# Low parts of the later batches' weights and keys: from GpSimd to VectorE

## The chip, the cores and the metric

The kernel runs on one core of a Trainium2 chip. The metric is the time of one execution on the device in microseconds (us); lower is better. Engines are named as in the profile: PE is TensorE, DVE is VectorE, ACT is ScalarE, POOL is GpSimd, SP is SyncE, which issues most of the transfers.

## The reference

Four batches of 576 positions pass through three layers one after the other: attention with 8 heads of 64, which keeps only scores close to the row's largest; a channel layer with a low-rank mixing of positions in front of it; and a layer of 8 experts, to which each position is routed.

```python
scores = q @ k.T / sqrt(64)                     # 4 batches, 8 heads, 576 x 576
scores = where(scores >= max(scores) - tau, scores, -1e9)
x = softmax(scores) @ v                         # heads side by side: 576 x 512
u = x + (x.T @ U @ V).T                         # rank 32, over positions
x = u + relu(u @ w_ch1) @ w_ch2                 # 512 -> 2048 -> 512
e[s] = argmax(x @ w_gate) or the expert of the position before   # by x @ w_local
out = p[e] * relu(x @ w1[e]) @ w2[e]            # 512 -> 1024 -> 512
```

All of it is in float32, and the outputs have to stand close to that.

## The kernel before

**High and low parts.** A float32 operand of a matrix product is split in two: `hi` is the value rounded to the format that PE multiplies fast (an ACT copy into a tile of that type), `lo` is the rest, a subtraction `x - hi` on another engine. A product is then three matmuls: hi times hi, hi times lo, lo times hi. Low parts that read a product's result in PSUM are made on DVE (`hl` at line 618). Two kinds of low part read two tiles in SBUF, and stand on POOL: those of the channel layer's weights (`w0l` and `w1l`, line 598, 128x512) and those of the keys (`kl`, line 268, 128x576 and 128x640), the latter but for the first pair of heads, which has them on DVE.

**The loops.** `attention(b)` goes over 4 pairs of heads, and in each over 5 groups of rows. For a group PE makes two tiles of scores `s`, DVE takes their maximum (line 326) and the threshold `st` (line 330, two numbers a row), ACT the exponential (line 337), DVE masks (line 341), and PE transposes the result and multiplies it by the values. `load_pair` brings the next pair's keys and queries. `channel(b)` goes over 16 blocks f of the hidden layer. `mlp_l1` makes `l` tiles of 256 and 320 columns from 12 matmuls each; ACT writes `hh` from one, DVE writes `hl` from it, and then the PSUM bank is free. After each fourth block `mlp_l2` adds four blocks up (lines 631 to 633), and DVE adds the result to `yT` (line 634). `load_w(b, f)` is called two blocks ahead: two transfers, two roundings on ACT (line 597), two low parts on POOL. `w0` has two buffers of each part, `w1` five, the raw `wr` six. The `l` tiles share two PSUM banks with the tiles of the router (`route`: `row`, `bk`, `cnt`) and of the stores (`py`); during the last batch's channel layer every third of them has one of two further banks.

**What runs together.** The first batch's attention runs alone. Then `attention(b)` and `channel(b-1)` are interleaved for b = 1, 2, 3, together with the router and the stores of batch b-2. At the end `channel(3)` runs beside `early_slots`, which sorts the positions of the first three batches by expert (DVE work on small tiles: `ssta`, `oha`, `rha`, and PE's `pia`, line 865, 10 columns). Then come the experts.

**What sets the order.** Nearly all of the program is written as generators, and a scheduler puts each engine's instructions into one static order from its own estimates of their durations; each engine works through its own list in order. Only POOL during the first batch's attention, and SP during the experts, keep the order of the code. `LAST` holds the last `w0l` subtraction; the first gather of the experts, which POOL issues, is put behind it.

Of the kernel before, what the change touches and what calls it, by code (L numbers as in the profile page):

```python
# [8 lines left out]
F32 = mybir.dt.float32  # L9
# [6 lines left out]
ALU = mybir.AluOpType  # L16
# [4 lines left out]
B, H, S, D = 4, 8, 576, 64  # L21
# [62 lines left out]
def attention_channel_moe(ctx, tc, qk, vv, tau, umat, vrep, wch, wgl, wexp, consts, out):  # L84
    nc = tc.nc
    pe, dve, act, pool, sp = nc.tensor, nc.vector, nc.scalar, nc.gpsimd, nc.sync
# [152 lines left out]
    def load_pair(b, hp, later=None):  # L239

        i = b * NPAIR + hp
# [4 lines left out]

        cuts = ((0, 0, 128), (1, 0, S), (0, 704, 832), (1, S, QKW), (0, 128, 704), (0, 832, QKW)) if i == 0 else (
            (1, 0, S), (1, S, QKW), (0, 0, 608), (0, 608, QKW))
        eng = pool if i else dve
        def steps():  # L250
            for n, (kq, c0, c1) in enumerate(cuts):
                c = slice(c0, c1)
# [243 lines left out]
    def attention(b):  # L496
        prev = None
        nxt = load_pair(b, 0)
        for hp in range(NPAIR):
            inp = nxt  # L500
            if hp + 1 < NPAIR:
                nxt = load_pair(b, hp + 1)
            for g in range(5):
                fr = front(b, hp, g, inp)
                yield 1.0
                if prev is not None:
                    yield from with_chain(back(*prev))
                prev = (b, hp, g, inp, fr)
        yield from with_chain(back(*prev))
        while CHAIN:  # L510
            yield link()

    def attention_alone(b):

        pend, debt, loads = [], 0.0, []
        inps = {0: load_pair(b, 0)}
        seq = [(hp, g, h) for hp in range(NPAIR) for g in range(5) for h in range(1 if g == 4 else 2)]
        groups = {}
# [66 lines left out]
    def load_w(b, f):  # L585
        nm = f"{b}_{f}"
        if f >= NF or nm in W:
            return
        while DONE[0] < f:
            next(conv, None)  # L590
        r = []
        for i, bufs in ((0, W0), (1, W1)):
            x = mlp.tile([128, 512], F32, tag="wr", name=f"wr{nm}_{i}", bufs=WR)
            sp.dma_start(out=x, in_=wdram[f * 128:f * 128 + 128, i * 512:i * 512 + 512])
            hi = mlp.tile([128, 512], F32R, tag=f"w{i}h", name=f"w{i}h{nm}", bufs=bufs)
            lo = mlp.tile([128, 512], F32R, tag=f"w{i}l", name=f"w{i}l{nm}", bufs=bufs)
            act.activation(hi, x, AF.Copy)  # L597
            x = pool.tensor_tensor(out=lo, in0=x, in1=hi.bitcast(F32), op=ALU.subtract)  # L598
            if i == 0:
                LAST[:] = [x.ins]  # L600
            r.append((hi, lo))
        W[nm] = r
# [34 lines left out]
    def channel(b):  # L637
        hs = {}
        load_w(b, 0)
        load_w(b, 1)  # L640
        for f in range(NF):
            yield from mlp_l1(b, f, hs)
            if f % 4 == 0 and f:
                yield from mlp_l2(b, f - 4, hs)
            load_w(b, f + 2)
        HS[b] = hs
# [625 lines left out]
```

## Time and profile before

| | us |
|---|---|
| median of 3 runs | 1080.13 (1078.6 to 1081.64) |
| the profiled execution | 1076.96 |
| its span in the trace | 1075.1 |
| first batch's attention alone | up to about 120 |
| attention beside the channel layer | about 120 to 690 |
| last channel layer | about 690 to 790 |
| experts | from about 790 |

A timeline row has start, duration, engine, line, operation, tiles written <- read (buffer numbers left out), the shape where there is one, and the count. In square brackets is the engine's idle time before it and what ended it. A group row has the busy time, the mean duration in ns of one instruction, the idle time just before the group, and who ended that. A row of stretches has the stretch, its length, each engine's busy time with the number of instructions (PE, PEld, DVE, ACT, POOL), the granted PE clock, the share of the DMA engines and GB/s. PEld is the weight load of a matmul and overlaps PE.

### The profile page before, as it was taken

What the parts mean: (1) busy time and instruction counts of PE and PEld (TensorE: products, weight loads), DVE (VectorE), ACT (ScalarE), POOL (GpSimd) and SP (SyncE); (2) the same over time, 40 slices, a digit from 0 to 9 for tenths busy, and PEclk for the clock granted to TensorE, in tenths of its full rate; (3) what the DMA queues carried; (4) which work ended last, traced back from release to release, by engine and by line L of the source; (5) the groups of instructions that cost most, each with busy time, mean ns of one, the idle gap of its engine ahead of it and who ended that gap; (6) DMA issues with size and microseconds to landing.
All of it is one profiled execution on the core that took longest, in us unless ns stands there. A gap on an engine that the chain in (4) does not pass through costs nothing. (4 is left out here: it accounts for less than half of the span.)

```text
span 1075.1 us, 19235 instructions
## 1 busy us (share of the span) xinstructions
PE 1019.5 (95%) x7088; PEld 906.0 (84%) x7088; DVE 678.0 (63%) x1645; ACT 580.3 (54%) x1220; POOL 256.2 (24%) x206
## 2 busy tenths in 40 slices
PE   5789889999999999999899999999999999999996
PEld 4566779888887899888789998989999888988985
DVE  6899766775656566656565654474257865556773
ACT  5788775674656366474645555422245254445563
POOL 1222032241422133042313213213340140120110
PEclk9899999999999999999999999999999999999999
DMA  6645577872423132242312101253124584456650
GB/s 198 198 139 150 156 243 237 253 227 95 129 65 116 54 100 65 76 129 60 111 49 79 50 30 60 88 191 120 59 93 141 176 302 158 160 172 230 201 176 15
DMA packets 57989, 143.80 MB, mean 134 GB/s; under 512 B 7133, under 2 KB 7901, under 8 KB 57888
## 3 DMA queue, kind: packets, MB, share of 16 engines
q1 hardware_dynamic: 54528, 132.27, 39.1%
q0 software_dynamic: 3360, 10.23, 2.8%
q8 instruction: 57, 0.93, 0.3%
q14 instruction: 44, 0.36, 0.1%
HBM read 124.65 MB, written 18.61 MB: 133 GB/s over the span
## 5 line engine op out<-in xcount | busy, mean ns | idle before, releaser
L614 PE MATMUL l<-uh,w0h 128*128 128x256 f32 (+1 forms) x512 | 158.0, 309 | 4.5 <-DVE hl L618 4.1
L631 PE MATMUL l<-hh,w1h 128*128 128x256 f32 (+1 forms) x512 | 157.6, 308 | 0.2 <-DVE exia L814 0.2
L615 PE MATMUL l<-ul,w0h 128*128 128x256 f32 (+1 forms) x512 | 153.3, 299 | 0.0
L616 PE MATMUL l<-uh,w0l 128*128 128x256 f32 (+1 forms) x512 | 153.2, 299 | 0.0
L632 PE MATMUL l<-hl,w1h 128*128 128x256 f32 (+1 forms) x512 | 152.9, 299 | 0.0
L633 PE MATMUL l<-hh,w1l 128*128 128x256 f32 (+1 forms) x512 | 152.6, 298 | 0.0
L598 POOL TENSOR_TENSOR w1l<-wr,w1h 128x512 fp32r<-128x512 f32 x64 | 82.0, 1304 | 281.5 <-ACT w1h L597 242.8
L598 POOL TENSOR_TENSOR w0l<-wr,w0h 128x512 fp32r<-128x512 f32 x64 | 83.4, 1302 | 244.8 <-ACT w0h L597 223.8
L337 ACT ACTIVATE p<-s,st 128x576 f32<-128x576 f32 x144 | 104.4, 740 | 63.0 <-DVE st L326 62.8
L1022 ACT ACTIVATE eh<-ew 128x512 fp32r<-128x512 f32 x160 | 94.1, 627 | 74.3 <-PE el L1138 43.2
L1023 DVE TENSOR_TENSOR el<-ew,eh 128x512 fp32r<-128x512 f32 x160 | 106.5, 691 | 37.9 <-ACT eh L1022 36.4
L341 DVE SCALAR_TENSOR_TENSOR p<-s,st,p 128x576 f32<-128x576 f32 x144 | 114.6, 815 | 16.0 <-ACT p L337 10.4
L326 DVE TENSOR_REDUCE st<-s 128x1 f32<-128x576 f32 x144 | 105.5, 751 | 26.3 <-PE s L293 24.4
L291 PE MATMUL s<-kh,qs 128*128 128x288 f32 x320 | 99.8, 330 | 16.5 <-DVE p L341 6.7
L390 ACT ACTIVATE ptt<-tp 128x512 f32<-128x512 f32 (+1 forms) x192 | 90.2, 492 | 39.9 <-PE tp L389 39.5
L634 DVE TENSOR_TENSOR yT<-l,yT 128x256 f32<-128x256 f32 (+1 forms) x128 | 58.3, 455 | 81.4 <-PE l L633 80.9
L618 DVE SCALAR_TENSOR_TENSOR hl<-l,hh 128x256 fp32r<-128x256 f32 (+1 forms) x128 | 58.1, 454 | 79.3 <-ACT hh L617 78.5
L614 PEld LDWEIGHTS l<-uh,w0h 128*128 128x128 f32 x512 | 97.4, 190 | 7.9 <-DVE hl L618 5.3
L631 PEld LDWEIGHTS l<-hh,w1h 128*128 128x128 f32 x512 | 97.5, 190 | 3.7 <-issue 2.4
L389 PE MATMUL tp<-cst,p 128*128 128x128 f32 x576 | 94.1, 280 | 5.5 <-ACT ptt L390 5.3
L632 PEld LDWEIGHTS l<-hl,w1h 128*128 128x128 f32 x512 | 97.5, 190 | 0.6
L615 PEld LDWEIGHTS l<-ul,w0h 128*128 128x128 f32 x512 | 97.4, 190 | 0.4
(443 smaller groups left out, 2397.6 us busy)
## 6 DMA issues: line engine op xcount, KB each, us to landing
ew<-in_wexp_dram SPq DMA_DIRECT2D x80, 512.0 KB, 4.6
wr<-wdram SPq DMA_DIRECT2D x128, 256.0 KB, 3.0
cr<-in_wch_dram SPq DMA_DIRECT2D x32, 512.0 KB, 5.1
raw<-in_qk_dram SPq DMA_DIRECT2D x30, 304.0 KB, 3.3
wdram<-w SPq DMA_DIRECT2D x32, 256.0 KB, 2.7
v<-in_vv_dram SPq DMA_DIRECT2D x16, 352.0 KB, 3.3
raw<-in_qk_dram SPq DMA_DIRECT2D x16, 320.0 KB, 3.7
raw<-in_qk_dram SPq DMA_DIRECT2D x17, 288.0 KB, 3.3
```

The costliest lines, as they stand in the source:

```text
L291: pe.matmul(s["t"][:, h, :288], lhsT=qs[:, qc:qc + 128], rhs=kh[:, k0:k0 + 288], start=(j == 0), stop=False)
L326: dve.tensor_reduce(out=self.st[:, 0, h:h + 1], in_=self.t[h], axis=AX.XY, op=ALU.max, negate=True)
L337: act.activation(self.halves(h), self.t[h], AF.Exp, bias=self.st[:, 0, h:h + 1])
L341: dve.scalar_tensor_tensor(out=p, in0=self.t[h], scalar=self.st[:, 1, h:h + 1], in1=p, op0=ALU.is_ge, op1=ALU.mult, accum_out=self.rvs[:, ...
L598: x = pool.tensor_tensor(out=lo, in0=x, in1=hi.bitcast(F32), op=ALU.subtract)
L614: pe.matmul(pm, lhsT=w1h[:, wk], rhs=uh[:, k, o:o + n], start=(k == 0), stop=False)
L615: pe.matmul(pm, lhsT=w1h[:, wk], rhs=ul[:, k, o:o + n], start=False, stop=False)
L616: pe.matmul(pm, lhsT=w1l[:, wk], rhs=uh[:, k, o:o + n], start=False, stop=(k == 3))
L631: pe.matmul(pm, lhsT=w2h[:, wd], rhs=hh[:, o:o + n], start=(f == f0), stop=False)
L632: pe.matmul(pm, lhsT=w2h[:, wd], rhs=hl[:, o:o + n], start=False, stop=False)
L633: pe.matmul(pm, lhsT=w2l[:, wd], rhs=hh[:, o:o + n], start=False, stop=(f == f0 + 3))
L1023: dve.tensor_tensor(out=lo, in0=x, in1=hi.bitcast(F32), op=ALU.subtract)
```

## The change

The subtraction that makes a low part is put on DVE in more places. For the weights: all blocks of `channel(1)` and `channel(2)` (2 x 16 blocks x 2 = 64) and the first 8 blocks of `channel(3)` (16), 80 in all; batch 0 and the last 8 blocks stay on POOL. For the keys: the pairs of batches 2 and 3 (2 x 4 pairs x 2 = 16). The instructions themselves, their tiles and their buffers are the same, and so is the last `w0l`, which stays on POOL ahead of the gather.

```diff
@@ load_pair
-        eng = pool if i else dve
+        eng = dve if i == 0 or b > 1 else pool
@@ load_w
-            x = pool.tensor_tensor(out=lo, in0=x, in1=hi.bitcast(F32), op=ALU.subtract)
+            eng = dve if b and (b < B - 1 or f < 8) else pool
+            x = eng.tensor_tensor(out=lo, in0=x, in1=hi.bitcast(F32), op=ALU.subtract)
```

The added line moves all lines behind it by one: line 598 becomes 599, and 618 becomes 619. The scheduler makes new orders. Three places of them follow; in the names `l_1_3_256` is the l tile of batch 1, block 3, columns from 256 on, and `hl_3` the low part of block 3's hidden values; `p_0_4` is pair 0, group 4 of the attention that runs beside it; `l_3_0_1_256` is a tile of batch 3's `mlp_l2`.

DVE where `channel(1)` has come to block 3, in the kernel before (at 336 to 342 us of its trace):

```order
L729 COPY seq_3705<-bk_4006 96x1
L730 SCALAR_TENSOR_TENSOR rsm_3704<-seq_3705,rsm_3704 96x6
L732 TENSOR_TENSOR e_all<-cst,rsm_3704 96x48
L341 SCALAR_TENSOR_TENSOR p_0_4_4078,rv_0_0_3637<-s_0_4_0_4080,st_0_4_4079,p_0_4_4078 128x576
L618 SCALAR_TENSOR_TENSOR hl_3_3971<-l_1_3_0_3972,hh_3_3970 128x256
L733 TENSOR_TENSOR rbig_3706<-e_all,rbig_3706 96x48
L351 TENSOR_SCALAR rv_0_0_3637<-rv_0_0_3637 128x1
L272 SCALAR_TENSOR_TENSOR qs_4141<-raw_2_4152,t_63,qs_4141 64x608
L734 TENSOR_REDUCE rsm_3704<-rbig_3706 96x6
L352 RECIPROCAL rv_0_0_3637<-rv_0_0_3637 128x1
L735 TENSOR_TENSOR tw_all<-rsm_3704 96x6
L618 SCALAR_TENSOR_TENSOR hl_3_3971<-l_1_3_256_4014,hh_3_3970 128x320
```

And DVE there in the changed kernel; the first of the pair's two `kl` stands one row ahead of these:

```order
L730 COPY seq_3705<-bk_4006 96x1
L330 TENSOR_SCALAR st_0_4_4079<-st_0_4_4079,t_63 128x1
L731 SCALAR_TENSOR_TENSOR rsm_3704<-seq_3705,rsm_3704 96x6
L268 TENSOR_TENSOR kl_4143<-raw_1_4148,kh_4142 128x640
L619 SCALAR_TENSOR_TENSOR hl_3_3971<-l_1_3_0_3972,hh_3_3970 128x256
L733 TENSOR_TENSOR e_all<-cst,rsm_3704 96x48
L341 SCALAR_TENSOR_TENSOR p_0_4_4078,rv_0_0_3637<-s_0_4_0_4080,st_0_4_4079,p_0_4_4078 128x576
L734 TENSOR_TENSOR rbig_3706<-e_all,rbig_3706 96x48
L351 TENSOR_SCALAR rv_0_0_3637<-rv_0_0_3637 128x1
L272 SCALAR_TENSOR_TENSOR qs_4141<-raw_2_4152,t_63,qs_4141 64x608
L735 TENSOR_REDUCE rsm_3704<-rbig_3706 96x6
L619 SCALAR_TENSOR_TENSOR hl_3_3971<-l_1_3_256_4014,hh_3_3970 128x320
```

The keys' low parts now stand in DVE's own list. The first `hl_3` has moved ahead of the mask (line 341), and the second stays behind line 272 but ahead of line 352.

DVE in `channel(1)` around block 0, ahead of the low part `hl_0` of columns 256 on, before (at 313 to 316 us):

```order
L341 SCALAR_TENSOR_TENSOR p_0_1_3728,rv_0_0_3637<-s_0_1_0_3730,st_0_1_3729,p_0_1_3728 128x576
L723 TENSOR_SCALAR cr_3721<-row_3720 1x96
L341 SCALAR_TENSOR_TENSOR p_0_1_3728,rv_0_0_3637<-s_0_1_1_3736,st_0_1_3729,p_0_1_3728 128x576
L724 SCALAR_TENSOR_TENSOR cr_3721<-cr_3721,row_3720 1x96
L351 TENSOR_SCALAR rv_0_0_3637<-rv_0_0_3637 128x4
L352 RECIPROCAL rv_0_0_3637<-rv_0_0_3637 128x4
L618 SCALAR_TENSOR_TENSOR hl_0_3680<-l_1_0_256_3747,hh_0_3679 128x320
```

And in the changed kernel:

```order
L599 TENSOR_TENSOR w1l_4_3967<-wr_4_1_3964,w1h_4_3966 128x512
L724 TENSOR_SCALAR cr_3721<-row_3720 1x96
L341 SCALAR_TENSOR_TENSOR p_0_1_3728,rv_0_0_3637<-s_0_1_0_3730,st_0_1_3729,p_0_1_3728 128x576
L725 SCALAR_TENSOR_TENSOR cr_3721<-cr_3721,row_3720 1x96
L341 SCALAR_TENSOR_TENSOR p_0_1_3728,rv_0_0_3637<-s_0_1_1_3736,st_0_1_3729,p_0_1_3728 128x576
L599 TENSOR_TENSOR w0l_2_3780<-wr_2_0_3777,w0h_2_3779 128x512
L619 SCALAR_TENSOR_TENSOR hl_0_3680<-l_1_0_256_3747,hh_0_3679 128x320
```

Two weights' low parts have come in, one of them just ahead of `hl_0`, and lines 351 and 352 have moved behind it.

PE in `channel(3)` where the first `pia` stands, before (at 714 to 717 us):

```order
L631 MATMUL l_3_0_1_256_8658<-hh_0_8241,w1h_0_8225 128x320
L632 MATMUL l_3_0_1_256_8658<-hl_0_8242,w1h_0_8225 128x320
L633 MATMUL l_3_0_1_256_8658<-hh_0_8241,w1l_0_8226 128x320
L631 MATMUL l_3_0_1_256_8658<-hh_1_8309,w1h_1_8237 128x320
L865 MATMUL pia<-rha_8569,r1a_8570 128x10 x2
L632 MATMUL l_3_0_1_256_8658<-hl_1_8310,w1h_1_8237 128x320
L633 MATMUL l_3_0_1_256_8658<-hh_1_8309,w1l_1_8238 128x320
L865 MATMUL pia<-rha_8591,r1a_8592 128x10 x2
```

And in the changed kernel:

```order
L634 MATMUL l_3_0_2_0_8681<-hh_0_8241,w1l_0_8226 128x256
L632 MATMUL l_3_0_1_256_8658<-hh_0_8241,w1h_0_8225 128x320
L633 MATMUL l_3_0_1_256_8658<-hl_0_8242,w1h_0_8225 128x320
L634 MATMUL l_3_0_1_256_8658<-hh_0_8241,w1l_0_8226 128x320
L632 MATMUL l_3_0_1_256_8658<-hh_1_8309,w1h_1_8237 128x320
L633 MATMUL l_3_0_1_256_8658<-hl_1_8310,w1h_1_8237 128x320
L634 MATMUL l_3_0_1_256_8658<-hh_1_8309,w1l_1_8238 128x320
L632 MATMUL l_3_0_1_256_8658<-hh_2_8369,w1h_2_8305 128x320
L633 MATMUL l_3_0_1_256_8658<-hl_2_8370,w1h_2_8305 128x320
L634 MATMUL l_3_0_1_256_8658<-hh_2_8369,w1l_2_8306 128x320
L632 MATMUL l_3_0_1_256_8658<-hh_3_8445,w1h_3_8365 128x320
L866 MATMUL pia<-rha_8569,r1a_8570 128x10 x2
```

The first `pia` has moved behind six more matmuls of `l_3_0_1_256` and three of the next tile, and both `pia` of the first two `rha` stand close together after it.

## Rows read from the trace of the kernel before

**Rows 1.** The page: span, and each engine's busy time and share.

```profile
span 1075.1 us, 19235 instructions
...
PE 1019.5 (95%) x7088; PEld 906.0 (84%) x7088; DVE 678.0 (63%) x1645; ACT 580.3 (54%) x1220; POOL 256.2 (24%) x206
```

**Rows 2.** Stretches: the loop of batches 1 to 3, and what follows.

```profile
250.00:690.00 440.00, 430.10 (x3229) 385.07 (x3228) 255.34 (x637) 237.41 (x516) 115.91 (x89) 1.00 0.25 76
690.00:745.00 55.00, 52.51 (x388) 51.38 (x388) 31.96 (x133) 18.69 (x40) 17.13 (x14) 0.97 0.50 173
```

**Rows 3.** Groups by line on POOL, 250 to 745 us.

```profile
L598 POOL TENSOR_TENSOR w0l<-wr,w0h 128x512 fp32r<-128x512 f32 x44 | 56.7, 1288 | 156.1 <-ACT w0h L597 148.9 <-PE l L616 4.4 <-DMA ydram<-yr 2.8
L598 POOL TENSOR_TENSOR w1l<-wr,w1h 128x512 fp32r<-128x512 f32 x44 | 55.9, 1295 | 197.3 <-ACT w1h L597 197.3
L268 POOL TENSOR_TENSOR kl<-raw,kh 128x576 fp32r<-128x576 f32 (+1 forms) x14 | 20.7, 1501 | 8.2 <-ACT kh L267 8.2
```

**Rows 4.** Single lines and tiles on DVE: duration in ns, least/median/most.

```profile
L1023 DVE TENSOR_TENSOR el<-ew,eh x160: 652/683/1533, 720.5 to 1055.3; 128x512 fp32r<-128x512 f32 x160
L268 DVE TENSOR_TENSOR kl<-raw,kh x2: 757/792/826, 5.9 to 8.3; 128x576 fp32r<-128x576 f32 x1, 128x640 fp32r<-128x640 f32 x1
L330 DVE TENSOR_SCALAR st<-st,t x44: 212/228/1066, 250.9 to 659.6; 128x2 f32<-128x2 f32 x35, 128x1 f32<-128x1 f32 x9
L730 DVE TENSOR_TENSOR_SCAN rsm<-seq,rsm x4: 226/894/1562, 336.1 to 823.4; 96x6 f32<-96x6 f32 x4
```

**Rows 5.** Groups by line and shape on DVE, 250 to 745 us.

```profile
L330 DVE TENSOR_SCALAR st<-st,t 128x2 f32<-128x2 f32 x35 | 12.3, 350 | 0.8
```

**Rows 6.** Waits of PE, 250 to 790 us: total, times, longest.

```profile
PE l L614 <- DVE hl L618: 4.1, 4, 1.1
...
PE s L291 <- DVE p L341: 0.8, 4, 0.2
```

**Rows 7.** Timeline, 333 to 343 us, POOL, DVE and PE.

```profile
334.64 2.96 POOL L268 TENSOR_TENSOR kl<-raw,kh 128x576 fp32r<-128x576 f32 x2 [0.26 <-ACT kh L267]
...
336.06 1.56 DVE L730 TENSOR_TENSOR_SCAN rsm<-seq,rsm 96x6 f32<-96x6 f32 x1
...
338.52 0.42 DVE L618 SCALAR_TENSOR_TENSOR hl<-l,hh 128x256 fp32r<-128x256 f32 x1
...
338.85 1.26 DVE L733 TENSOR_TENSOR rbig<-e_all,rbig 96x48 f32<-96x48 f32 x1
...
338.99 0.38 PE L614 MATMUL l<-uh,w0h 128*128 128x256 f32 x1 [0.89 <-DVE hl L618]
...
341.41 0.48 DVE L618 SCALAR_TENSOR_TENSOR hl<-l,hh 128x320 fp32r<-128x320 f32 x1
...
341.94 0.41 PE L614 MATMUL l<-uh,w0h 128*128 128x320 f32 x1 [1.15 <-DVE hl L618]
```

**Rows 8.** Timeline, 312 to 317 us, DVE and PE.

```profile
312.87 0.82 DVE L341 SCALAR_TENSOR_TENSOR p<-s,st,p 128x576 f32<-128x576 f32 x1
...
315.89 0.49 DVE L618 SCALAR_TENSOR_TENSOR hl<-l,hh 128x320 fp32r<-128x320 f32 x1 [0.77 <-ACT hh L617]
...
316.44 0.38 PE L614 MATMUL l<-uh,w0h 128*128 128x256 f32 x1
```

**Rows 9.** Timeline, 713 to 725 us, PE.

```profile
715.08 0.31 PE L631 MATMUL l<-hh,w1h 128*128 128x320 f32 x1
...
716.45 0.61 PE L865 MATMUL pia<-rha,r1a 96*128 96x10 f32 x4 [1.06 <-DVE rha L882]
```

**Rows 10.** Stretches of 5 us around it.

```profile
715.00:720.00 5.00, 3.94 (x25) 3.68 (x24) 3.98 (x24) 1.78 (x3) 0.00 (x0) 0.83 0.87 317
720.00:725.00 5.00, 5.00 (x35) 5.00 (x35) 3.31 (x15) 0.00 (x0) 0.00 (x0) 0.82 1.02 403
725.00:730.00 5.00, 5.00 (x42) 5.00 (x42) 3.44 (x9) 2.24 (x5) 2.68 (x2) 1.00 0.10 38
```

**Rows 11.** Timeline, 696 to 699 us, ACT, DVE and PE.

```profile
696.69 0.63 ACT L597 ACTIVATE w0h<-wr 128x512 fp32r<-128x512 f32 x1 [1.02 <-PE l L615]
...
697.68 0.49 DVE L618 SCALAR_TENSOR_TENSOR hl<-l,hh 128x320 fp32r<-128x320 f32 x1 [2.26 <-ACT hh L617]
...
698.80 0.39 PE L614 MATMUL l<-uh,w0h 128*128 128x320 f32 x1
```

## The prediction, made before the changed kernel ran

> **What bounds the kernel now.** I read the page's engine line first: PE is busy for 1019.5 of 1075.1 us, 95%, DVE for 63%, POOL for 24% [rows 1]. Then the table of stretches, because the change acts between about 233 us (the first weights of `channel(1)`) and 740 us only: from 250 to 690 us PE is busy for 430.10 of 440 us at the full granted clock, DVE for 255.34; from 690 to 745 us it is 52.51 of 55 and 31.96 [rows 2]. The reader is to see that PE sets the pace, with 9.9 + 2.5 = 12.4 us of idle in those 495 us, and that DVE has 184.7 + 23.0 = 207.7 us free. Whatever the change gives can only come out of these 12.4 us and out of stretches at half clock; what it costs has to come as new waits of PE. So third the waits of PE, to see who holds it: for DVE's `hl` 4 times, 4.1 us in all, for the masked `p` 4 times, 0.8 us [rows 6]. No wait of PE for `w0l`, `w1l` or `kl` stands among them. Nobody on PE is late because POOL makes the low parts slowly; POOL itself waits 148.9 and 197.3 us for ACT's rounding [rows 3]. So the shorter duration on DVE is by itself worth nothing, and the time is decided at the few places where DVE is what PE waits for.
>
> **What moves.** On POOL a weight's low part takes 1.29 us, a key's 1.50 us [rows 3]. On DVE the trace before has no weight's low part, but the experts' line 1023 is the same operation on the same shape and types, all in SBUF: 0.683 us median; and the first pair's `kl` is on DVE, 0.79 us [rows 4]. So DVE takes over 80 x 0.683 + 16 x 0.792 = 54.6 + 12.7 = 67.3 us. It fits in the 207.7 us that are free; DVE goes from 58% to about 72% of the stretch. In sum it is hidden, under matmuls that keep PE busy. Not hidden is what stands just ahead of an instruction that PE waits for. On POOL 64 + 16 weights' and 16 keys' parts go away. The roundings on ACT and all transfers keep their place in the code, and SP gets no new wait: a `wr` buffer comes free earlier if anything, and there are six. The new wait is DVE's for ACT's rounding: POOL could stand in it for free, DVE holds all behind it, `hl` and masks above all. The new order puts these instructions behind roundings that are long done as the scheduler reckons; I take 0 for that wait itself, and a late rounding is part of the slow rival.
>
> **Term A, DVE is held less by POOL: a gain.** A DVE instruction that works from SBUF to SBUF while POOL works takes much longer: line 330 needs 228 ns at the median and 1066 at most, line 730 226 and 1562, line 1023 683 and 1533 [rows 4]. Over all 35 of line 330 with two columns that is 35 x (350 - 228) = 4.3 us of DVE time [rows 5]. It counts only where PE waits behind it. One such place is the router's step at 336 us: POOL makes two `kl` (334.64 to 337.60); line 730 takes 1.56 and line 733 1.26 us, the two `hl` come late, and PE waits 0.89 and 1.15 us for them [rows 7]. In the changed kernel the keys of this pair are on DVE itself, 0.8 us each, one of them ahead of the first `hl`, which has moved ahead of the mask. Going through the new order with 0.79 for `kl`, and 0.23 and 0.21 for lines 731 and 734, I get the later of the two tiles started at about 340.75 instead of 341.94: -1.2 us. The next batch has the same step with the same order: A = 2 x -1.2 = -2.4 us. The bounds are 0 and both waits gone, 2 x -2.04 = -4.1.
>
> The Trainium skill ("Perfetto Trace Analysis", section Optimizing Scalar/DVE Operations) says that GpSimd and DVE share a read port of SBUF, so that moving work from one to the other might not help. That is a rule against this change; the stretched instructions agree that the two hold each other up, and whether that is the port no run here shows. Taken as "nothing is won by moving", it makes A nothing, and the sum below +1.0, that is 1081.1.
>
> **Term B, weights ahead of `hl` in `channel(1)`, block 0: a loss.** Before, DVE's `hl` at 315.89 us started as soon as ACT's `hh` was there, after 0.77 us of idle, and PE's next tile of that bank at 316.44, right behind its end [rows 8]. So each 0.1 us of delay is PE's. Now a `w1l` stands ahead of the masks and a `w0l` just ahead of this `hl`: 2 x 0.69 = 1.4 us, of which the idle of 0.77 takes the larger part, and lines 351 and 352 have moved behind. That makes +0.6, or +1.3 where the second stands late; I take +0.9, and 2 x 0.9 = +1.8 us with the twin in the next batch. The bounds are 0 and +2.6.
>
> **Term C, the last channel layer: a gain.** The first `pia` made PE wait for 1.06 us [rows 9]. It has moved behind 9 more matmuls, six of 320 columns and three of 256; at the spacing of the trace, 0.147 and 0.119, that is 1.24 us. Taking the last of them as ahead of `rha` by a part only, 0.8 us of the 1.06 go. Around this stall the granted clock falls: 0.83 and 0.82 in two stretches of 5 us, then 1.00 [rows 10]; in between, from about 718 to 722 us, matmuls follow each other at 0.21 instead of 0.12 us, half the clock. That costs about 1.5 us, and I count it as gone with the stall. Against that, the tile `bk` of the router moves 4 matmuls back, behind a `w0l`: +0.5 (0 to 1.1). C = -0.8 - 1.5 + 0.5 = -1.8; with the clock unchanged -0.3.
>
> The Trainium skill ("TensorE: Matmul & The Clock Gate", section HAM oscillation) has the clock go down after idle of PE. That the fall here comes behind the stall agrees; by that rule a new pause at the place of term B could bring the half clock there too, at 1.5 us for each of the two batches, and the sum would become -1.4 + 3.0 = +1.6, that is 1081.7.
>
> **Term D, `w0l` right ahead of other `hl`.** In the new order about 16 of the 80 stand directly ahead of an `hl` of 320 columns, and push it by about 0.69 - 0.36 = 0.33 us each, where 0.36 is DVE's mean idle there: at most 5.3 us. Mostly the tile that wants the bank is not there yet: at 697.68 us such an `hl` ends at 698.17, and its successor starts at 698.80, which leaves 0.63 of room, with the rounding of `w0h` already over at 697.32 [rows 11]. That PE waits for `hl` only four times in 540 us [rows 6] says that room is the rule. I take +1.0. The mask, with one or two `kl` ahead of it in the new order, comes 0.9 to 1.1 us later in some groups; PE waits for masks only 0.8 us in all [rows 6], and has other tiles to go on with. I take 0 there (at most 1).
>
> **The sum.** -2.4 + 1.8 - 1.8 + 1.0 = -1.4 us. The profiled execution took 1076.96, 1.86 more than its span, and would become 1075.6; it lies 3.2 us below the median of 1080.13, for which I forecast 1078.7. About 0.3%, 3.2 us, is what a measurement can tell from no change, so this is a forecast of no measurable change.
>
> **The rivals.** *Faster.* Only the gains are real: the static order absorbs B, D and `bk`, as it does nearly everywhere else, and the held `hl` waits of A go in full or nearly so. Then it is -2.4 - 0.8 - 1.5 from A and C, and another -1.1 from the single waits (the rest of A's, one of 0.4 us behind a held line 330): -5.8, 1074.3. For it speaks that all waits of PE for DVE lie where POOL is at work, against it that the new order shows `w0l` and `w1l` just where there was little room.
>
> *Slower.* A bank of an `l` tile is freed by `hl`, and DVE works in order. If the `w0l` ahead of `hl`, together with a mask behind its `kl`, is over the room, PE waits at most blocks: 16 x 0.33 = 5.3 from D, 2.6 from B, 1.1 from `bk`, less A's half (-1.2) and C's stall (-0.8): +7.0, 1087.1. It decides from where `hl` ends later than PE's next use of the bank, 0.63 us after `hl`'s end in the example [rows 11] and none at B [rows 8]. A late rounding on ACT acts just so, since DVE then stands as POOL does now [rows 3]. For it speaks that DVE gets 26% more work in an order that its instructions can't leave; against it, that DVE still has 28% idle and that a tile of `l` takes PE over 1.5 us, more than twice a `w0l`.
>
> *It doesn't do what it says:* a weight's part on DVE could take not 0.69 but the 1.53 of the longest line 1023 [rows 4], if batch 0's weights or batch 1's keys on POOL ran beside it. But POOL then has little left in this stretch, and I give it no chance of its own; where it happens it is the slow rival.
>
> **How the numbers follow.** The forecast (-1.4, itself from -3.2 to +3.2) gets 0.46, faster 0.33, slower 0.21. The two unknown signs, B and D against A and C, all hang on a microsecond here and there, which is why no case holds more than half. The range: down to the faster case and a little under its 1074.3, 1073.5; up to 1085.0, which takes in two thirds of the slow case and leaves out its end of 1087.1. Faster by over 0.3%: 0.33; within: 0.46; slower: 0.21.
>
> **What would show it.** In the profile of the changed kernel: DVE about 67 us busier less the held time (some 14 us), so near 730 us; `w0l` and `w1l` at 0.68 to 0.70 us. Term A: lines 731 and 734 at 0.2 us, and PE's wait for the second `hl_3` near 0. Term B: PE's wait for `hl` at 313 to 318 us near 0.9. Term C: the granted clock at 1.00 in both stretches of 5 us from 715 on, and the first `pia` without a wait over 0.3. Term D: PE's waits for `hl` over the whole stretch within 3 to 6 us. I am wrong if these waits grow past 8 us (the slow rival), if they fall under 1 (the faster one), or if the time moves by over 3 us with PE's waits for DVE unchanged: then the cause lies in something I have not priced, the order of PE itself or transfers.

## The result and the profile after

The changed kernel took 1068.26 us (median of 4 runs, 1064.99 to 1068.99) against 1079.37 of the kernel before (4 runs): a ratio of 0.9898, 95% interval 0.9878 to 0.9919, or 11 us faster. A second measurement, beside other kernels, gave 0.9915 (0.9894 to 0.9937). The forecast was 1078.7, no measurable change, and its range ended at 1073.5: the time lies below it. The direction was that of the "faster" rival, and about twice as far.

The page of the changed kernel, span and engine line; the lines before are in [rows 1]:

```profile
span 1065.9 us, 19218 instructions
...
PE 1015.5 (95%) x7088; PEld 903.9 (85%) x7088; DVE 718.0 (67%) x1741; ACT 580.0 (54%) x1220; POOL 131.7 (12%) x110
```

DVE has become 40 us busier, not 67: it does 67 us more, is held some 15 us less (counted below), and its consecutive instructions overlap by 12 us more, which the busy time counts once. The share of PE stays at 95%: over the whole span its busy time fell by 4.0 us and its idle time by 5.2. The two stretches of [rows 2], now:

```profile
250.00:690.00 440.00, 436.10 (x3281) 392.89 (x3280) 297.46 (x739) 239.97 (x524) 6.13 (x5) 1.00 0.25 79
690.00:745.00 55.00, 54.95 (x419) 54.17 (x418) 32.36 (x131) 16.50 (x35) 5.90 (x5) 1.00 0.47 161
```

PE's idle is 3.9 + 0.05 = 3.95 us, where it was 12.4. All waits of PE from 250 to 790 us that are left, to be read beside [rows 6]:

```profile
PE row L723 <- DVE seq L721: 1.3, 2, 0.9
PE tp L389 <- ACT ptt L390: 1.2, 3, 0.5
PE s L291 <- DVE p L341: 0.4, 2, 0.2
```

The waits for `hl` (4.1 us) are gone, and so are those for `bk` (1.25) and `pia` (1.06, [rows 9]), and one for `yT`. Two of these rows in the kernel before:

```profile
PE bk L728 <- DVE cr L724: 1.3, 1, 1.3
...
PE pu L466 <- DVE yT L468: 0.8, 2, 0.4
```

On DVE the durations of [rows 4] and [rows 5] have become the following: the moved low parts (groups by line and shape, 250 to 745 us), and the lines that were held up (the two columns' form of line 330 as a group, the router's two lines each with least/median/most):

```profile
L599 DVE TENSOR_TENSOR w1l<-wr,w1h 128x512 fp32r<-128x512 f32 x40 | 27.6, 709 | 3.8 <-ACT w1h L597 3.7
L599 DVE TENSOR_TENSOR w0l<-wr,w0h 128x512 fp32r<-128x512 f32 x40 | 27.5, 688 | 19.5 <-ACT w0h L597 17.7 <-PE tp L395 1.6
L330 DVE TENSOR_SCALAR st<-st,t 128x2 f32<-128x2 f32 x35 | 7.9, 225 | 0.6
L731 DVE TENSOR_TENSOR_SCAN rsm<-seq,rsm x4: 219/223/226, 335.9 to 813.3; 96x6 f32<-96x6 f32 x4
L734 DVE TENSOR_TENSOR rbig<-e_all,rbig x4: 198/202/204, 338.0 to 814.1; 96x48 f32<-96x48 f32 x4
```

Hardly anything on DVE is stretched any more: line 330 has a mean of 0.225 us where it was 0.350, and the scan needs at most 0.226 where it was 1.56.

### The profile page after: what moved, and what is told of

Read it like the earlier page. It is cut to its first block, busy times and chain, and to the rows that moved or that the text cites. A ratio compares the mean times of both kernels' runs of the same rounds, so it can differ in the third digit from the quotient of the medians.

```text
span 1065.9 us, 19218 instructions
## 1 busy us (share of the span) xinstructions
PE 1015.5 (95%) x7088; PEld 903.9 (85%) x7088; DVE 718.0 (67%) x1741; ACT 580.0 (54%) x1220; POOL 131.7 (12%) x110
## 5 line engine op out<-in xcount | busy, mean ns | idle before, releaser
L599 POOL TENSOR_TENSOR w1l<-wr,w1h 128x512 fp32r<-128x512 f32 x24 | 31.8, 1342 | 543.0 <-ACT w1h L597 522.5
L617 PEld LDWEIGHTS l<-uh,w0l 128*128 128x128 f32 x512 | 97.8, 191 | 0.2
L634 PEld LDWEIGHTS l<-hh,w1l 128*128 128x128 f32 x512 | 96.8, 189 | 0.2 <-issue 0.2
```

Source lines behind the costliest of these rows:

```text
L617: pe.matmul(pm, lhsT=w1l[:, wk], rhs=uh[:, k, o:o + n], start=False, stop=(k == 3))
L634: pe.matmul(pm, lhsT=w2l[:, wd], rhs=hh[:, o:o + n], start=False, stop=(f == f0 + 3))
```

## Where the time went

For the comparison of traces I took the start of the same matmul (the n-th of the first layer's) in two traces. The table gives by how many us it starts later than in the kernel before, at places named by the time in that kernel's trace. Up to about 250 us the change does next to nothing on VectorE, and what differs there differs between executions; so the last column is the move from 276 to 784 us. The rows contain what an execution lost to the half clock. From 250 to 790 us the kernel before, the changed kernel, e5 and e13 have one stretch at half clock each, worth 1.7 us; e2, e3, e6 and e14 have two, e4 three. Rows with different numbers of them can't be compared to closer than that.

| kernel | 276 | 339 | 376 | 467 | 567 | 689 | 732 | 784 | 276 to 784 |
|---|---|---|---|---|---|---|---|---|---|
| changed kernel | +1.1 | -1.2 | -3.2 | -3.4 | -5.5 | -5.3 | -9.8 | -9.8 | -10.9 |
| e2 no low parts | +2.6 | +1.6 | -0.4 | -0.5 | -3.2 | -3.2 | -7.7 | -7.7 | -10.3 |
| e3 keys only | +3.6 | +3.3 | +1.4 | +1.3 | -1.3 | -1.3 | -1.6 | -1.6 | -5.2 |
| e4 weights of batches 1, 2 | 0.0 | +0.5 | -1.1 | -0.6 | -0.5 | -0.1 | -0.7 | -0.7 | -0.7 |
| e5 weights of batch 3 | +0.2 | +0.5 | +0.5 | +0.5 | +0.6 | +0.8 | -3.7 | -3.7 | -3.9 |
| e6 GpSimd loaded beside | +1.5 | +0.7 | -0.2 | +1.3 | +4.3 | +8.4 | +6.7 | +7.5 | +6.0 |
| e13 the same, fewer pieces | +1.7 | +0.5 | -0.9 | -0.3 | -0.8 | +0.4 | -3.0 | -3.0 | -4.7 |
| e14 the same with copies | +1.5 | +0.8 | -1.1 | -0.9 | -2.2 | -1.4 | -5.3 | -5.3 | -6.8 |

The gain of the changed kernel comes in three steps: around the router's step of 336 us, around its twin of 530 us, and in the first blocks of the last channel layer, 697 to 732 us. The router's step in the kernel before has a row of POOL that [rows 7] leaves out:

```profile
338.76 1.29 POOL L598 TENSOR_TENSOR w0l<-wr,w0h 128x512 fp32r<-128x512 f32 x1 [1.17 <-ACT w0h L597]
```

So the scan (line 730) ran beside the second `kl`, and `rbig` (line 733) beside a weight's low part, not beside a key's. Each ended with the GpSimd instruction beside it: the scan at 337.62 and the `kl` at 337.60, `rbig` at 340.11 and the `w0l` at 340.05. That is so nearly everywhere: of the 17 DVE instructions from 250 to 745 us that take over 0.3 us longer than their median in the changed kernel, 15 end 0.02 to 0.06 us behind the end of a GpSimd instruction. So, as far as these ends show, VectorE does not work more slowly there; it is held until GpSimd's instruction is over.

## The experiments

Three theories stood against each other. **Theory 1**: GpSimd's work beside VectorE lengthens VectorE's instructions, and the gain is that this work is gone. **Theory 2**: the gain is the new static order. **Theory 3**: the raw tiles come free earlier, so that SyncE's queue is not held. The comparisons are with the kernel before on the same chip.

### e2: the low parts left out

```diff
+            if eng is dve:
+                r.append((hi, hi))
+                continue
```

and the same for the keys (`kl = kh`), with the orders nearly those of the kernel before.

> The kernel before, with the 96 low parts that the change moves left out: the matmuls read the high part in their place, so that part of the computation is missing, while TensorE does the same number of matmuls. GpSimd has no such work and VectorE has none more; the orders are nearly those of the kernel before. Theory 1 (GpSimd holds VectorE up): the gain is there without the new order, 1066 to 1071 us, and the four waits for hl are gone. Theory 2 (the new order): 1077 to 1080 us, with the waits for hl of about 4 us still there.

The whole time, 1095.13 us (1.014, 1.0119 to 1.0162), can't be used: with the wrong low parts other positions go to other experts, and the experts' part has 60 more matmuls (7148 against 7088 in all). Up to 790 us the two kernels do the same matmuls, and there the table shows -10.3 us. The two stretches and PE's waits from 250 to 790 us:

```profile
250.00:690.00 440.00, 437.20 (x3275) 393.72 (x3274) 249.41 (x654) 239.94 (x524) 6.37 (x5) 0.99 0.26 79
690.00:745.00 55.00, 55.00 (x422) 54.31 (x421) 27.70 (x124) 17.30 (x36) 5.18 (x4) 1.00 0.48 164
```

```profile
PE tb L445 <- DVE xsd L437: 0.7, 2, 0.4
PE tp L392 <- ACT ptt L393: 0.5, 2, 0.3
PE s L294 <- DVE p L344: 0.4, 2, 0.2
PE row L729 <- DVE seq L727: 0.2, 1, 0.2
PE py L686 <- DVE rv L354: 0.2, 1, 0.2
```

No wait for `hl`, `bk` or `pia`, with the first `pia` behind the same number of second-layer matmuls as before and the order nearly the old one: without the low parts, at least 1202 of VectorE's 1231 instructions up to 780 us stand in the same sequence as before; in the changed kernel it is 1154. Theory 2 falls: the new order is not needed for the gain. Theory 3 is not tested by this run, since the raw tiles come free earlier here too. The changed kernel gains about as much (-10.9); PE idles 3.95 us in its two stretches and 2.8 here, so the 67 us on VectorE cost about 1 us.

### e6, e13, e14: GpSimd loaded again, the order kept

In e6 GpSimd does work beside each moved low part that nobody needs and that frees no raw tile (shortened; `scratch` stands for a tile of one buffer):

```diff
             x = eng.tensor_tensor(out=lo, in0=x, in1=hi.bitcast(F32), op=ALU.subtract)
+            if eng is dve:
+                for j in (0, 256):
+                    pool.tensor_tensor(out=scratch, in0=hi.bitcast(F32)[:, j:j + 256], in1=cst[:, j:j + 256], op=ALU.subtract)
```

For the keys there are three pieces of 192 columns. e13 has one piece (keys: two), e14 has copies, `pool.tensor_copy(out=scratch, in_=hi...)`, in place of the subtractions.

> The changed kernel with GpSimd loaded as before, but with work that frees no buffer: behind each of the 96 low parts it subtracts a constant from the rounded operand, in two or three pieces, into a scratch tile that nobody reads. The orders of TensorE and VectorE are word for word those of the changed kernel. Theory 1 (GpSimd's work beside VectorE lengthens VectorE's instructions): 1075 to 1083 us, VectorE 15 to 30 us busier between 250 and 745 us, TensorE waits again for hl; waits of SyncE's loads on GpSimd play no part. Theory 2 (the order): 1067 to 1070. Theory 3 (the raw buffers come free earlier, and SyncE's queue with the stores behind those loads moves on earlier): 1067 to 1070 too, since no load waits for GpSimd here.

e6 took 1084.68 us: 1.0060 of the kernel before (1.0044 to 1.0076), 16 us over the changed kernel with the very same orders of TensorE and VectorE. Theories 2 and 3 expected none of this. The orders of PE, DVE and ACT in the traces of e6, e13 and e14 are instruction for instruction those of the changed kernel, and ACT's instructions take the same time in all of them (the roundings 0.63 and 0.62 us). Groups on DVE from 250 to 745 us, and on POOL the load (lines 602, 333 and 344 are 599, 330 and 341 of the changed kernel):

```profile
L344 DVE SCALAR_TENSOR_TENSOR p<-s,st,p 128x576 f32<-128x576 f32 x79 | 62.3, 812 | 4.1 <-ACT p L340 1.5
L602 DVE TENSOR_TENSOR w1l<-wr,w1h 128x512 fp32r<-128x512 f32 x40 | 36.4, 928 | 3.7 <-ACT w1h L600 3.7
L602 DVE TENSOR_TENSOR w0l<-wr,w0h 128x512 fp32r<-128x512 f32 x40 | 32.7, 817 | 18.8 <-ACT w0h L600 18.7
...
L333 DVE TENSOR_SCALAR st<-st,t 128x2 f32<-128x2 f32 x35 | 10.5, 300 | 0.6
...
L605 POOL TENSOR_TENSOR scr<-w0h,cst 128x256 bf16<-128x256 f32 x80 | 71.9, 899 | 86.9 <-ACT w0h L600 82.7
```

Line 599's mean goes from 709 and 688 to 928 and 817 ns, line 330's from 225 to 300, while the mask, which reads PSUM, stays at 0.81 us. This is the stretching of [rows 4] again, though for the larger part on other instructions: the extra work stands beside the moved low parts by construction. One part of the expectation did not come: the waits for `hl` stayed small (0.8 us in all), and the router's scan takes at most 0.34 us here. PE's idle of 14.2 us (250 to 745) lies at other places, the largest rows being:

```profile
PE tp L392 <- ACT ptt L393: 4.3, 7, 1.4
PE pu L469 <- DVE th L465: 1.7, 3, 1.0
```

e6 loads GpSimd with 180 us between 250 and 745, where the kernel before had 133 [rows 2]. Therefore e13, which stays under that load, and e14 with the other form:

> As e6, with one piece (keys: two) of GpSimd work behind each low part in place of two (three), so that GpSimd is busy for some 85 to 110 us between 250 and 745 us, less than in the kernel before (133) where e6 had 180. The orders of TensorE and VectorE are word for word those of the changed kernel. Theory 1 with a loss in proportion to GpSimd's load: e6 lost 16 us for 168 us of load, so 8 us or so here, 1075 to 1079. If the loss of e6 came from its load above that of before only: 1067 to 1071.

> As e6, with a plain copy of the rounded operand in place of each piece's subtraction, so that GpSimd reads one operand and not two. If VectorE is held by any GpSimd instruction for as long as it runs: the loss goes with GpSimd's busy time (0.1 us for each us), 1075 to 1085, and lines 599 and 330 are lengthened as in e6. If what holds VectorE is GpSimd's second operand: 1067 to 1071, with those lines at 0.69 and 0.23 us.

e13 took 1073.93 us, 0.9978 of the kernel before (0.9960 to 0.9995), which lies between its two expectations and nearer to the first; e14 1070.93, 0.9947 (0.9928 to 0.9967). As "held" I count all that DVE's instructions from 250 to 745 us need above their median in the changed kernel, where it is over 0.1 us.

| | POOL busy, 250 to 745 us | DVE held | ratio to the kernel before |
|---|---|---|---|
| changed kernel | 12.0 | 1.3 | 0.9898 and 0.9915 |
| e14 copies | 119.2 | 5.8 | 0.9947 |
| e13 fewer pieces | 110.0 | 15.6 | 0.9978 |
| kernel before | 133.0 | 15.9 | 1 |
| e6 | 180.5 | 30.9 | 1.0060 |

The loss goes with the load, and starts below the load of the kernel before: by the ratios e13 gives back about three quarters of the gain, by the table of the traces a little over half (6.2 of 10.9 us). It goes even better with the held time. Of e13's 15.6 us, 8.7 fall on the moved low parts themselves; in the kernel before it was `st`, the scan and `rbig` that were held most. So these runs show that such work beside VectorE costs the kernel time in a fixed order; what stood at the router's step is shown by e2, e3 and e4. With nearly e13's load, copies hold DVE for little over a third of the time; a copy of 128x256 takes 0.57 us on POOL, a subtraction 0.9. So it is not any GpSimd work to the same degree: the form with two operands from SBUF holds DVE more. Not all of e14's loss is held time: GpSimd reads the rounded tile here, and ACT's next rounding waited for it for 4.3 us in e14 (0.4 in e6, not at all in e13). That a copy holds nothing, as one of the expectations had it, is wrong too: `w1l` and `w0l` have a mean of 768 and 720 ns there, against 709 and 688.

The Trainium skill ("SBUF — State Buffer", section Who interferes with whom) has a VectorE instruction with two inputs in SBUF, or a `tensor_scalar` in a two-port mode, contend with a GpSimd instruction that reads SBUF, and one with at most one SBUF input outside those modes not. The traces agree: beside GpSimd's work the low parts (up to 1.70 us in e6), the scan (1.56 before) and line 330 (1.07 before) are lengthened; `hl`, the mask and the maximum, which read PSUM, take at most 0.49, 0.82 and 0.76 us in all of them. Whether it is the port, no run here shows.

### e1: the same with buffers held

The same again, with the load as a subtraction into the raw tile (shortened: `pool.tensor_tensor(out=x0, in0=x0, in1=hi..., op=ALU.subtract)`), so that the tile comes free when GpSimd is done.

> The changed kernel, with a second subtraction on GpSimd behind each of the 96 that moved: it writes x - hi into the raw tile that VectorE has just read and that nobody reads any more. GpSimd is as loaded as before the change; VectorE's and TensorE's orders are those of the changed kernel but for a few rows. Theory 1 (the gain is that GpSimd no longer lengthens VectorE's instructions that work from SBUF to SBUF): most of the 11.1 us comes back, 1074 to 1079 us, lines 330 and 731 show durations of about 1 us again, and TensorE waits 3 us or more for hl. Theory 2 (the gain is the new order, in which hl, bk and pia stand elsewhere): 1068 us within 2 us, whatever the durations of those lines.

1092.7 us, 1.0130 (1.0109 to 1.0151), 24 us over the changed kernel and beyond what theory 1 expected. Its signs came: PE waits 5.8 us for `hl`, and the scan takes up to 1.20 us; line 330 takes up to 0.65, not 1. But GpSimd's load was 137 us and VectorE was held for 27.1 us by the count above, both less than in e6, and the loss was 8 us more. Theory 3's mechanism is at work here, as loads on SP's queue wait for raw tiles that GpSimd frees, and ACT for the keys' loads. From the waits of the queue and of ACT, 250 to 745 us:

```profile
SPq L596 <- POOL wr L603: 317.5, 77, 20.3
...
ACT qs L272 <- DMA raw<-in_qk_dram: 9.7, 7, 2.5
```

And from the queue's waits in the kernel before:

```profile
SPq L594 <- POOL w1l L598: 207.4, 44, 19.9
SPq L594 <- POOL w0l L598: 142.2, 42, 7.0
```

The queue waits for GpSimd in the kernel before about as long (349.6 us, against 317.5), so the queue's waits alone do not explain the 8 us. ACT's wait for the keys' loads is new (9.7 us, 1.5 before). What makes e1 so much slower stays open. For the change itself e6 and e13 show that the larger part comes without raw tiles being held. How much of the changed kernel's 11 us is owed to earlier freed `wr` tiles stays open too.

### e3, e4, e5: the change in parts

```diff
-            eng = dve if b and (b < B - 1 or f < 8) else pool
+            eng = pool                                        # e3: keys only
+            eng = dve if 0 < b < B - 1 else pool              # e4, keys as before
+            eng = dve if b == B - 1 and f < 8 else pool       # e5, keys as before
```

> The kernel before with the keys' low parts of the last two batches on VectorE alone, 16 of the 96. Theory 1: the GpSimd work beside the router's step at 336 us is two kl, so the four waits for hl go (-4.1 us), and little else: 1074 to 1076 us. Theory 2: the orders are nearly those of before, so within 2 us of the kernel before, 1077.5 to 1081.5.

> The kernel before with the weights' low parts of the second and third batch on VectorE alone, 64 of the 96. Theory 1: the keys stay on GpSimd and the waits for hl at 339 to 342 us with them; only line 330's waits (0.8 us) and small ones go: 1077 to 1079.5 us. Theory 2: the orders are for the larger part those of the changed kernel up to 690 us, so about 6 us of the gain are there: 1072 to 1075 us. Neither expects the gain of the last channel layer (bk, pia, clock), 4.3 us.

> The kernel before with the weights' low parts of the last batch's first 8 blocks on VectorE alone, 16 of the 96. After the runs so far (keys alone 5 us, the middle batches' weights about 1) what is left of the gain, about 4 us in the last channel layer, is due to these: 1074.5 to 1076.5 us, without waits for bk (1.25) and pia (1.06), and with the full granted clock from 715 to 725 us. If the keys or the middle weights are needed for it too, 1077.5 us or more.

e3: 1075.95 us, 0.9965 (0.9950 to 0.9980). e4: 1076.96, 0.9987 (0.9972 to 1.0002). e5: 1074.14, 0.9965 (0.9952 to 0.9977). PE's waits in e3 from 250 to 790 us have no `hl` any more, but `pia` and `bk`; in e5 it is the other way round. In e4 half of the `hl` waits are gone. The first three rows are e3's:

```profile
PE tp L389 <- ACT ptt L390: 1.5, 4, 0.5
PE pia L866 <- DVE rha L883: 1.0, 1, 1.0
PE bk L729 <- DVE cr L725: 1.0, 1, 1.0
```

then one of e5, and one of e4 with the router's step there:

```profile
PE l L615 <- DVE hl L619: 4.1, 4, 1.2
```

```profile
PE l L615 <- DVE hl L619: 1.8, 2, 0.9
...
336.60 1.56 DVE L731 TENSOR_TENSOR_SCAN rsm<-seq,rsm 96x6 f32<-96x6 f32 x1
...
339.39 0.19 DVE L734 TENSOR_TENSOR rbig<-e_all,rbig 96x48 f32<-96x48 f32 x1
```

Keys alone, 16 of 96 instructions, bring a third of the gain or a little more by the ratios and half by the table, because a `kl` ran just beside the router's scan [rows 7]; with the keys moved, no weight's low part falls beside `rbig` either. The weights of the last batch, another 16, bring 3.9 us in the last channel layer. The 64 of the middle batches bring nothing in the times that is clear of noise; theory 2 had put the gain there. But the expectation that all four waits stay was wrong: where the middle weights are moved and the keys are not (e4), the scan still takes 1.56 us and the first wait of each step stays, while `rbig`, which had stood beside a weight's low part, is back at 0.19 us and the second wait is gone.

By the ratios the three parts are 0.35, 0.13 and 0.35%, in sum 0.83, where the whole is 0.85 to 1.02%. The table's -5.2 - 0.7 - 3.9 = -9.8 us comes as near, but partly by luck: e3's execution lost 1.7 us more to the half clock than the kernel before, e4's 3.4 more, and the waits that e4 saves are among those that e3 saves.

### e7 to e12: does it go further?

```diff
-        eng = dve if i == 0 or b > 1 else pool
+        eng = dve if i == 0 or b > 0 else pool                            # e7, e10, e11, e12
+        eng = dve                                                         # e8
-            eng = dve if b and (b < B - 1 or f < 8) else pool
+            eng = dve if b and (b < B - 1 or f < NF - 1) else pool        # e7, e10
+            eng = dve if b < B - 1 or f < NF - 1 else pool                # e8
+            eng = dve if (b or f >= 5) and (b < B - 1 or f < NF - 1) else pool   # e11
```

> The changed kernel with, in addition, the keys of the second batch and 7 more blocks of the last batch's weights on VectorE (the last block stays on GpSimd). Theory 1 wins a little more, since GpSimd still works from 120 to 250 us (keys) and from 745 us on: 1065 to 1068 us. If VectorE becomes too full or the experts' start is disturbed: 1069 to 1073.

> As the run before it, and the first batch's channel weights on VectorE too (32 low parts, loaded while attention of the second batch runs). Theory 1: GpSimd's 39.7 us between 120 and 250 us go, and with them part of TensorE's idle of 4.8 us there: 1062 to 1066 us. If VectorE, which is busy for 71% of that stretch, now makes TensorE wait for masks: 1068 to 1074.

> The changed kernel as it is, beside the kernel before and the two that follow: 10 to 12 us under the kernel before. It is the measure for whether the next ones are faster than it.

> The kernel of e7 again (the changed kernel with the second batch's keys and 7 more blocks of the last batch's weights on VectorE): if its gain over the changed kernel is real, 1.5 to 3 us under it; if it was between chips, within 1 us.

> The kernel of e7 with the low parts of the first batch's blocks from the sixth on also on VectorE (22 low parts, from about 138 us on); e8 with all 32 lost 6 us before 122 us, in the first batch's attention, where VectorE is busiest, and nothing behind it. If only those early ones hurt, this one is at e7's time or up to 2 us under it; if VectorE is too full from 120 to 250 us as well, 2 to 5 us over it.

> The changed kernel with the second batch's keys on VectorE too, and none of the further weights. If e7's 2 us more come from 120 to 250 us, where GpSimd makes these keys' low parts, this is at e7's time; if they come from the last channel layer's second half, at the changed kernel's.

e7: 1066.02 us, 0.9889 (0.9874 to 0.9905); e8: 1073.65, 0.9954 (0.9938 to 0.9970). In the second group, side by side: e9 (the changed kernel) 0.9915 (0.9894 to 0.9937), e10 (e7's kernel) 0.9911 (0.9896 to 0.9925), e11 0.9923 (0.9905 to 0.9941), e12 0.9913 (0.9891 to 0.9935). The changed kernel's gain is 8.6 us here by the medians, where 10 to 12 were expected. The intervals lie over each other: none is shown to be faster than the changed kernel, and what seemed e7's 2 us was not there the second time. Only e8 is slower, by 7 us against e7. It does more than its expectation says: besides the first batch's weights it moves the low parts of the first batch's remaining keys, six in all. Up to 120 us, inside the first batch's attention, these six and five weights' low parts have gone to VectorE. The first 120 us of e7 and then of e8:

```profile
0.00:120.00 120.00, 91.92 (x583) 66.51 (x583) 101.70 (x247) 90.34 (x186) 17.03 (x17) 0.96 0.55 173
```

```profile
0.00:120.00 120.00, 92.71 (x553) 66.61 (x554) 100.00 (x247) 86.79 (x178) 1.19 (x6) 0.93 0.56 170
```

PE has got 30 matmuls less far, where VectorE is busy for 83% of the time. Much of that is an execution's own: with the granted clock at 0.93 there, e10, the kernel of e7, has got to 565 matmuls and e11 to 559, against e8's 553. The ratios still put e8 5 to 7 us behind e7's kernel. Whether the keys or the weights cost it is not shown: e11 leaves both these keys and the first five blocks' weights on GpSimd.

## Why the prediction was wrong

**What held.** PE is the bound, the gain came for the larger part (8.45 of 10.9 us) out of its 12.4 us of idle, the 67 us on VectorE were hidden but for about 1 us, and the low parts take 0.69 to 0.71 us. Nobody on PE had waited for POOL's results, and the cause I named under term A is the one that the runs show: e2 and e3 at the router's step, e6 and e13 with the order held fixed.

**Term A (forecast -2.4, bounds 0 and -4.1): -4.1.** All four waits are gone, in e3 too. The mechanism was right and the size was not: I had played through the new order with each delay of the old one partly kept. I had also put both long instructions down to the two `kl`; `rbig` ran beside a weight's low part, as e4 shows. The step at 336 us in the changed kernel (to be read beside [rows 7]):

```profile
336.07 0.81 DVE L268 TENSOR_TENSOR kl<-raw,kh 128x640 fp32r<-128x640 f32 x1
...
336.80 0.41 DVE L619 SCALAR_TENSOR_TENSOR hl<-l,hh 128x256 fp32r<-128x256 f32 x1
...
337.99 0.20 DVE L734 TENSOR_TENSOR rbig<-e_all,rbig 96x48 f32<-96x48 f32 x1
...
339.29 0.47 DVE L619 SCALAR_TENSOR_TENSOR hl<-l,hh 128x320 fp32r<-128x320 f32 x1
...
339.82 0.41 PE L615 MATMUL l<-uh,w0h 128*128 128x320 f32 x1
```

I expected that last matmul at 340.75. It is there at 339.82, without a wait. (Up to this step the two traces are 0.1 us apart.)

**Term B (forecast +1.8): 0. This step failed: that a `hl` pushed back by a low part makes PE wait.** The `w0l` did push `hl`, from 315.89 to 316.25 us, as I had reckoned:

```profile
315.64 0.69 DVE L599 TENSOR_TENSOR w0l<-wr,w0h 128x512 fp32r<-128x512 f32 x1 [0.22 <-ACT w0h L597]
...
315.88 0.59 ACT L682 ACTIVATE yr<-py 96x512 f32<-96x512 f32 x1
...
316.25 0.49 DVE L619 SCALAR_TENSOR_TENSOR hl<-l,hh 128x320 fp32r<-128x320 f32 x1
...
316.52 0.39 PE L615 MATMUL l<-uh,w0h 128*128 128x256 f32 x1
```

But the next `l` tile starts at 316.52, before this `hl` has ended (316.74): it stands in the bank that `yr` freed at 316.47. In the static order the first matmul of that tile waited for VectorE before, and waits for ScalarE now. `l` tiles and the tiles of router and stores share two banks in turn, so a new order also deals the banks anew. I had carried the pair of [rows 8] over as if it were fixed, though the waits stand in the order and could have been read.

**Term C (forecast -1.8): -2.3, and a clock that says nothing.** `pia`'s wait of 1.06 us is gone, -0.8 forecast. `bk` I had at +0.5 for its place in the list; its wait of 1.25 us went. Before, VectorE's `cr` was late for a store: SP's load waited until POOL's `w0l` had ended at 694.62 us, and the store of a `yr` that was ready at 694.05 stood behind it; the next `yr` and then `cr` waited for stores. Rows of the kernel before, POOL, SP, ACT, DVE and PE:

```profile
693.33 1.29 POOL L598 TENSOR_TENSOR w0l<-wr,w0h 128x512 fp32r<-128x512 f32 x1 [3.22 <-ACT w0h L597]
693.47 0.58 ACT L681 ACTIVATE yr<-py 96x512 f32<-96x512 f32 x1
694.65 0.32 SPq L594 DMA_DIRECT2D wr<-wdram  x1
695.06 0.95 SPq L683 DMA_DIRECT2D ydram<-yr  x2
...
700.31 0.59 ACT L681 ACTIVATE yr<-py 96x512 f32<-96x512 f32 x1 [2.66 <-DMA ydram<-yr]
...
703.15 0.06 DVE L721 MEMSET cr<- 1x1 f32 x1 [1.52 <-DMA ydram<-yr]
```

I had written that a raw tile comes free "earlier if anything" and gave it no price. That this alone made `bk` late isn't shown: e13 has 1.2 us of wait for `bk`, though GpSimd holds no raw tile of these blocks.

The half clock at 715 to 725 us [rows 10] is gone there, but I counted its 1.5 us as a gain, and it is none. The changed kernel lost as much at 495 us (5 us at a granted clock of 0.66, that is 1.7 us), and its second execution (e9) at 310 us instead. There it does not stand behind a stall, as I had read it in the kernel before: in both it begins right behind the router's twelve `lg` matmuls of 9 columns, at 495.23 and 309.42 us, without a wait of PE. The pauses at term B, for which I had set another 3.0 us of half clock, did not come. Stretches of the changed kernel, then of e9:

```profile
715.00:720.00 5.00, 5.00 (x42) 5.00 (x41) 4.57 (x15) 2.20 (x4) 0.96 (x1) 1.00 0.65 260
...
495.00:500.00 5.00, 5.00 (x30) 4.97 (x30) 3.42 (x18) 1.11 (x3) 0.00 (x0) 0.66 0.02 7
```

```profile
310.00:315.00 5.00, 5.00 (x32) 4.85 (x31) 3.66 (x18) 1.70 (x4) 0.00 (x0) 0.72 0.09 24
```

**Term D (forecast +1.0): 0. This step failed with B.** DVE's idle before the `hl` of 320 columns, 35.0 us in 44 of them (250 to 745 us), went down to 6.2: the low parts took just the time in which VectorE waited for ACT's `hh`. That could have been read before: 35.0 us in 44 is a mean of 0.80 us, more than the 0.69 of a `w0l`, and no row shows the 0.36 that I reckoned with. In the new order 24 `w0l` stand directly ahead of such an `hl`, not 16. (The slow rival's 26% more work for DVE is 23% over the 495 us in which it falls, 67.3 of 287.3 us.) PE waits for `hl` nowhere.

**And waits that I had left out:** 0.8 us for `yT` at line 466, which e3 and e5 still have and the changed kernel not, and 0.4 of the 0.8 for masks; 1.0 us for ACT's `ptt` at lines 408 and 389 went too.

**The sum.** 4.1 + 1.25 + 1.06 + 0.8 + 0.4 + 1.0 = 8.6 us of waits are gone, which is the 8.45 us by which PE's idle shrank but for rounding; the forecast was -1.4 in all. The largest misses are the two losses that did not come, B and D with +2.8, and A, 1.7 us too small. From 276 to 784 us the gain is 10.9, with the same loss by the clock in both; the 2.4 that are not idle in the profile's sense must lie in closer matmuls, and I have not found where. My errors have one root, as far as I can see. I charged VectorE's new work against the slack of the old profile at each place, while the same change gave VectorE 15 us back, part of it just where it was late; and I took losses that a list of instructions suggests as likely as gains that a row of waits shows.

The rule of the Trainium skill that I set against the change ("Perfetto Trace Analysis", Optimizing Scalar/DVE Operations: a shared port, so that moving work between GpSimd and VectorE might not help) did not hold as a forecast: 1081.1 by it, 1068.3 measured. That the two engines' work collides did hold: e6 shows GpSimd holding VectorE up. It costs time while both work; here most of GpSimd's work went (133 us down to 12, 250 to 745 us).

## What to carry to other kernels

Work on GpSimd is not free for a kernel that doesn't wait for its results: look at the longest duration of VectorE's small SBUF instructions beside their median, and at whose waits stand behind the long ones. Where they stand before the engine that bounds the kernel, it can pay to do the work on VectorE itself if VectorE has idle time, and a few instructions at the right place (16 keys of 96) may bring a third of the gain or more. And before a pushed instruction is charged to the bound, read from the order what its consumer now waits for: a new order deals shared buffers anew.

## What the runs showed that I had not expected

With the same orders, GpSimd's two-operand subtractions cost 0.07 to 0.1 us of kernel time for each us of GpSimd (e13: 7 to 9 us for 98 more than in the changed kernel, e6: 16 to 17 for 168), copies 0.03 to 0.05, part of which is ACT waiting for the rounded tile. VectorE was held for about twice as long as the kernel lost (15.6 and 30.9 us). What holds VectorE is a wait for the end of GpSimd's instruction and not a slower pace, so a scan of 96x6 can go from 0.22 to 1.56 us; in e6, 22 of the 28 low parts that were held for over 0.3 us end 0.55 us behind the end of one of GpSimd's. And a stretch at half clock, worth 1.7 us, comes behind one of the router's `lg` steps in one execution and behind another in the next: from 250 to 790 us the changed kernel's two executions had one each, the two of e7's kernel none, e6 two and e4 three.
